# Decay rows kept feature by feature in DRAM, and a v load behind their reads, in gated linear attention with a multiplicative FFN

## The chip, the cores and the metric

One core of one Trainium2 chip runs the kernel. The metric is device microseconds of one execution. The kernel before took 466.35 us, the median of 3 runs (466.15 to 468.48).

## What is computed

Two blocks follow each other. The first is gated linear attention: 4 batches of 8 heads, 768 steps, 48 features. Each head carries a state of 48 x 48:

```python
for t in range(S):
    state = alpha[:, :, t, :, None] * state + einsum('bhd,bhe->bhde', k[:, :, t], v[:, :, t])
    y[:, :, t] = einsum('bhd,bhde->bhe', q[:, :, t], state)
```

The second takes the result as 3072 tokens of 384 features and computes `((x @ w1) * (x @ w2)) @ w3 @ w_out`, with 1024 inner features. All data is float32 (the four weights come as float64).

## The kernel before

**Chunks.** The 768 steps of a batch are cut into 6 chunks of 128, so there are 24 chunks (n = 0 to 23) for all heads at once. Per chunk, alpha, k, q and v are loaded as tiles of 128 steps x 8 heads x 48 features (192 KB each); ScalarE takes the logarithm of alpha (L318, L326), TensorE sums it along the steps (L346, L352, L355), and ScalarE makes two exponentials of the sums, e[:, 0] = exp(-sum) (L361) and e[:, 1] = exp(sum) (L362). e has two buffers. VectorE scales k and q with them (L371). TensorE then turns k and q (L393), makes the scores (L510, later L476), VectorE masks them (L513, L483), and TensorE multiplies scores by v (L536, L436), the state by q (L530, L436), and k by v for the new state (L405), which VectorE adds to the old one (L413, L415).

**Two chunks on one base.** Sums of an even and the odd chunk before it run towards a common point, so that the state needs to be decayed only at even chunks. The even chunks 2, 4, 8, 10, 14, 16, 20 and 22 (those that don't begin a batch) have an entry in `ends`, a DRAM tile of 3 rows of 384 values: row 0 is the first row of exp(-sum) of chunk n (L364), row 1 the last row of exp(sum) of chunk n-1 (L366), row 2 the first row of alpha of chunk n (L322, L333). The product of the three is the decay of each of the 384 features. The state lies with the features on partitions, four heads on partitions 0 to 47 and four on 64 to 111, so the rows have to be turned: they are stored to DRAM, and two loads (L379, one for each half i) read them back with the feature d on the partition and 3 x 4 single values (row m, head pair j) on each. GpSimd multiplies the three (L422, L423) and scales the state: `Ts[0] = T(n-1) * dec` (L424).

**Queues.** All stores to `ends` and the loads from it are issued by GpSimd, in one order with its other work: chunk 3 to 7's v loads (L160), copies of v to the other half of the partitions (L168) and, late in the kernel, other transfers. A store waits for ScalarE's exponential, the loads wait until the three stores have landed, and L422 waits until the loads have landed. SP issues all other transfers, with raw weights (L238) and k and q (L154, L155) in between, each waiting for its buffer.

**Order.** The order of the program is written out by hand in the loop over n (L740 on): what an engine does next is the order in which it is called, with `after_marks`, which lets a piece of work be placed after a marked instruction. `mark["pool"]` is the newest store to `ends` or the newest L424; before chunk 6, chunk n + 2's v is issued after it (L776 to L778). In the first six chunks ScalarE and VectorE also convert the weights from float64 (L246 to L267). From chunk 6 on, the FFN's products (L566), three passes for each product in reduced precision, fill TensorE beside the attention, and from 184 us on they are alone.

Of the kernel before, what the change touches and what calls it, by code (L numbers as in the profile page):

```python
# [10 lines left out]
FP32 = mybir.dt.float32  # L11
# [37 lines left out]
def kernel(  # L49
# [12 lines left out]
    nc = tc.nc  # L62
    B, H, S, D = q.shape
    C = 128
    DM = H * D
    DF = moe_w1.shape[1]
    NCH = S // C
    N = B * NCH
    NP = H // 2
    DP = 64  # L70
# [15 lines left out]
    def pool(name, bufs, stack=ctx, **kw):  # L86
        return stack.enter_context(tc.tile_pool(name=name, bufs=bufs, **kw))
# [7 lines left out]
    dram = pool("dram", 1, space=DRAM)  # L95
# [14 lines left out]
    st, mark = {}, {}  # L110

    def after_marks(*names):
        stack = ExitStack()
        for x in names:
            stack.enter_context(tc.issue_after(mark[x]))
        return stack
# [1 line left out]

    ends = {n: dram.tile([3, DM], FP32, name=f"ends{n}") for n in range(2, N, 2) if n % NCH}
    xd = [dram.tile([DM, TG], FP32, name=f"xd{g}") for g in range(NG)]
    abd = [dram.tile([C, KF, TG], FP32, name=f"abd{g}") for g in range(NG)]

# [11 lines left out]
    def paired(n):  # L136
        return 2 <= n < PAIRED
# [12 lines left out]
    def load_kq(n):  # L150
        if n >= N:
            return
        st["kq", n] = inp.tile([C, 2, H, D], FP32, tag="kq", name="kq")
        nc.sync.dma_start(out=st["kq", n][:, 0], in_=rows(k, n))  # L154
        nc.sync.dma_start(out=st["kq", n][:, 1], in_=rows(q, n))  # L155

    def load_v(n):
        if n < N:
            st["v", n] = vs[n % len(vs)]
            (nc.gpsimd if 2 < n < 8 else nc.sync).dma_start(out=st["v", n][:, :, 0:D], in_=rows(v, n))  # L160
# [37 lines left out]
    decs = [p1.tile([C, 3, NP], FP32, name=f"dec{i}") for i in range(2)]  # L198
# [83 lines left out]
    def fetch(ahead=3):  # L282
        while weights and len(begun) < ahead:
            begun.append(weights.popleft())
            next(begun[-1])
# [17 lines left out]
    def store():  # L303

        while later:
            dst, src = later.popleft()
            nc.sync.dma_start(out=dst, in_=src)

    def last(n):
        return n % NCH == NCH - 1  # L310

    def logs(n):
        if n >= N:
            return
        a = st.pop(("a", n))
        if paired(n):
            if n % 2 == 0:
                nc.scalar.activation(a, a, AF.Ln)  # L318
                st["la", n] = st["la", n + 1] = a
                b, c = divmod(n, NCH)  # L320
                if n in ends:
                    nc.gpsimd.dma_start(out=ends[n][2:3].rearrange("m (h d) -> m h d", h=H), in_=alpha[b:b + 1, :, c * C, :])  # L322
            return
        a = a.rearrange("p h d -> p (h d)")
        la = st["la", n] = work.tile([C, DM], FP32, tag="la", name="la")
        nc.scalar.activation(la, a, AF.Ln)  # L326
        if n >= LATE:

            t = st["la", n] = work.tile([C, 2, DM], FP32R, tag="la2", name="la2", bufs=1)
            nc.scalar.copy(t[:, 0], la)  # L330
            nc.vector.tensor_sub(t[:, 1], la, t[:, 0].bitcast(FP32))
        if n in ends:
            nc.gpsimd.dma_start(out=ends[n][2:3], in_=a[0:1])  # L333

    def decays(n):
        if n >= N:
# [21 lines left out]
    def exponentials(n, lc):  # L358

        e = st["e", n] = work.tile([C, 2, DM], FP32, tag="e", name="e", bufs=2)  # L360
        nc.scalar.activation(e[:, 0], lc, AF.Exp, scale=-1.0)  # L361
        mark["e", n] = nc.scalar.activation(e[:, 1], lc, AF.Exp).ins  # L362
        if n in ends:
            mark["pool"] = nc.gpsimd.dma_start(out=ends[n][0:1], in_=e[0:1, 0]).ins  # L364
        if n + 1 in ends:
            mark["pool"] = nc.gpsimd.dma_start(out=ends[n + 1][1:2], in_=e[C - 1:C, 1]).ins  # L366
        load_ends(n)

    def decayed(n):
# [4 lines left out]
    def load_ends(n):  # L374
        if n not in ends:
            return
        with nc.allow_non_contiguous_dma(reason="single values to partitions"):
            for i in range(2):
                nc.gpsimd.dma_start(out=decs[n // 2 % 2][ds(DP * i, D)].rearrange("d m j -> d (m j)"),  # L379
                                    in_=ends[n].rearrange("m (j i d) -> i d (m j)", i=2, d=D)[i])  # L380

    def transposed(n):
        if n >= N:
# [166 lines left out]
    def load_x(g, queue=nc.sync):  # L550
        st["xT", g] = xp.tile([C, KM, TG], FP32, tag="xT", name="xT")
        queue.dma_start(out=st["xT", g], in_=xd[g].rearrange("(k p) t -> p k t", p=C))
# [171 lines left out]
    with after_marks(("e", 0)):  # L724
        logs(1)
# [14 lines left out]
    for n in range(N + 1):  # L740
        if n > TURNED:
            load_v(n + 2)
        if not 1 < n < FIRST:
            store()
        if n in loads:
            load_x(loads[n])
        if n != 1 and not 2 < n <= FIRST:
            load_a(n + 5)
        raws = (3, 3, 3, 3, 2, 2, 3, 3)[n] if n < 8 else 4
        for m in (n + 3,) * (n <= FIRST) + (n + 4,) * (n >= FIRST):  # L750
            load_kq(m)
            if 2 < n <= FIRST and m == n + 3:
                load_a(n + 5)
            if 1 < n < FIRST:
                store()
            if n < FIRST - 2:
                fetch(raws)
        if FIRST <= n <= TURNED:
            load_v(n + 2)
        if 0 < n <= TURNED:  # L760
            attend_state(n - 1)
        if n < TURNED:
            scores(n)
        else:
            attention(n)
        if ("lc", n + (2 if n == 1 else 3)) in st:
            exponentials(n + (2 if n == 1 else 3), st.pop(("lc", n + (2 if n == 1 else 3))))
        transposed(n + 1)
        if n == 1:
            decays(3)  # L770
            load_a(6)
            with after_marks(("e", 3)):
                logs(4)
        if n == FIRST + 1:
            run(2)
        if n < FIRST:  # L776
            with after_marks("pool"):
                load_v(n + 2)  # L778
        if n - 2 in begin and n > FIRST:
            g, tiles = begin[n - 2]  # L780
            with after_marks(("ms", n), ("qkT", n + 1)):
                split_x(g, 0)
            fill.extend(gate(g, f) for f in tiles)
        if n == FIRST:
            with after_marks("l", ("qkT", n + 1)):
                split_x(0, 0)
            fill.extend(gate(0, f) for f in begin[n - 3][1])
        pieces = ((3, 3, 2, 0) if n > FIRST + 3 else (0, 3, 3, 0))[(n - FIRST) % 4] if n >= FIRST else 0
        if n == 0:
            with after_marks(("qkT", 0)):  # L790
                logs(2)
            decays(2)
            with after_marks(("e", 2)):
                logs(3)
        early, ready = n < FIRST, len(thirds) if n > 2 else n // 2
        marks = (*[("qkT", n + 1)] * (n < N - 1), *[("qk", n + 1), ("ms", n)] * early, *["x3"] * (n - 2 in begin and n > FIRST))
        if n < N - 2 and n != FIRST:
            with after_marks(*marks):
                convert(2 if early else 1, raws)
        advance(n)  # L800
        turn_v(n)
        if n > TURNED:
            st.pop(("x", n - 1))()
        elif n:
            attend(n - 1)
        outer(n)
        if n > FIRST:
            third(ready)
        run(pieces > 0)
        if early:  # L810
            with after_marks(*marks):
                convert(1, raws)
        with after_marks(*[("ms", n)] * (n < 3)):
            decayed(n + 2)
        if not early:
            with after_marks(*[("qkT", n + 1)] * (n < N - 4)):
                logs(n + 4)
        if n == 4:
            load_x(0)
        convert(early and n > 0, raws)  # L820
        run(pieces > 1)
        if n:
            decays(n + 3)
        if n <= FIRST:
            third(ready)
        if 0 < n < FIRST:
            with after_marks(("e", n + 3)):
                logs(n + 4)
        if n == FIRST:
            with after_marks("x3", ("e", n + 3)):  # L830
                convert(2, raws)
        elif n < N - 2:
            convert(n == FIRST - 1 if early else n % 3 == 0, raws)
        if n == FIRST - 1:
            assert len(done) == 2 * KM
        run(pieces > 2)
        if n == N - 3:
            while begun:
                convert(1)
            weights.extend(load_out(j) for j in range(KF))  # L840
            fetch(4)
# [90 lines left out]
```

## Time and profile before

| | |
|---|---|
| median of the runs | 466.35 us |
| the profiled execution, its time | 463.35 us |
| the profiled execution, its span | 461.6 us |
| busy: TensorE, VectorE, ScalarE, GpSimd | 444.5, 362.9, 278.0, 97.6 us |
| GpSimd waits for `dec<-ends` (L422) | 33.4 us in 8 times |
| GpSimd waits for `ends<-e` (L379) | 15.8 us in 7 times |
| DMA issues to landing: `v<-in_v_dram` from GpSimd | x5, 5.4 us |
| `kq<-in_q_dram` from SP | x24, 5.4 us |
| all DMA | 80.38 MB, 149381 packets |

The span runs from the first to the last instruction; the execution's own time is 1.75 us longer. In a line of the timeline the first number is the start, the second the duration in us, and in brackets stands how long the engine was idle before and what ended it. In the chain of waits a line is a piece of the chain that ended last. `SPq` is SP's issue of transfers, PEld is TensorE's load of weights.

### The profile page before, as it was taken

How to read it: one execution, taken by the hardware profiler on the slowest of the kernel's cores; microseconds unless marked ns; L12 is line 12 of the kernel's file. 1: busy time of each engine (PE TensorE's matmuls, PEld its weight loads, DVE VectorE, ACT ScalarE, POOL GpSimd, SP SyncE). 2: the span in 40 equal slices, each digit the busy share in tenths (PEclk: the TensorE clock that was granted, in tenths of full speed). 3: DMA queues.
4: the chain of work that ended last, by engine and by line, in shares of the span. 5: the costliest groups of instructions: out<-in, count | busy, mean ns of one | idle time of the engine just before them, and what ended most of it. 6: DMA issues, size and time to landing. Idle time of an engine off the chain costs nothing.

```text
span 461.6 us, 11168 instructions
## 1 busy us (share of the span) xinstructions
PE 444.5 (96%) x4296; PEld 424.3 (92%) x4296; DVE 362.9 (79%) x578; ACT 278.0 (60%) x544; POOL 97.6 (21%) x186
## 2 busy tenths in 40 slices
PE   4969899999999999999999999999999999999996
PEld 2657699989999999999999999999999999999996
DVE  2878996899868879999997999997543966776671
ACT  4758775857667564998866676764545433333430
POOL 6335152215431460121221202112010000000000
PEclk9979999999999999999999999999999999999999
DMA  9999999999998966658764436412115865665511
GB/s 177 262 191 237 263 222 209 236 209 213 172 197 180 213 165 210 181 190 252 210 211 143 150 127 176 149 51 87 51 53 157 253 201 174 184 184 158 161 51 53
DMA packets 149381, 80.38 MB, mean 174 GB/s; under 512 B 97904, under 2 KB 139120, under 8 KB 149328
## 3 DMA queue, kind: packets, MB, share of 16 engines
q1 hardware_dynamic: 143552, 64.44, 56.4%
q0 software_dynamic: 5776, 15.22, 10.9%
q8 instruction: 34, 0.56, 0.5%
q14 instruction: 19, 0.16, 0.1%
HBM read 57.58 MB, written 22.06 MB: 173 GB/s over the span
## 4 chain that ended last, share of the span: by engine, by line
PE 87%; DVE 4%; DMA 4%; ACT 2%; issue 1%; SPq 0%; DVEq 0%; ACTq 0%
PE bank L566 72%; PE bank L436 5%; DMA kq<-in_q_dram 3%; PE bank L393 3%; PE bank L476 2%; PE bank L405 2%; DMA ac<-in_alpha_dram 2%; PE bank L355 1%; DVE qk L371 1%; PE bank L352 1%; PE bank L536 1%; DVE ms L513 1%; PE bank L510 1%; DVE mant L253 0%; DVE power L254 0%
## 5 line engine op out<-in xcount | busy, mean ns | idle before, releaser
L566 PE MATMUL bank<-x,w 128*128 128x384 f32 x1152 | 209.4, 337 | 0.9 <-DVE ms L483 0.9
L566 PEld LDWEIGHTS bank<-x,w 128*128 128x128 f32 x1152 | 200.3, 188 | 2.3 <-DVE ms L483 1.4
L566 PE MATMUL bank<-w3o,ab 128*128 128x384 f32 x576 | 100.2, 336 | 0.0
L566 PEld LDWEIGHTS bank<-w3o,ab 128*128 128x128 f32 x576 | 99.9, 188 | 0.0
L591 ACT ACTIVATE bank<-bank 128x384 f32<-128x384 f32 x96 | 45.8, 478 | 40.7 <-PE bank L566 40.6
L575 ACT ACTIVATE t<-bank 128x384 f32<-128x384 f32 x64 | 31.3, 494 | 53.9 <-PE bank L566 53.9
L641 POOL DMA_DIRECT2D abd<-ab x45 | 25.8, 573 | 135.2 <-DVE ab L627 115.7
L692 DVE TENSOR_TENSOR ab<-abl,ab 128x1024 fp32r<-128x1024 f32 x24 | 29.4, 1224 | 12.4 <-ACT ab L691 12.3
L691 ACT ACTIVATE ab<-abl 128x1024 fp32r<-128x1024 f32 x24 | 25.5, 1061 | 20.4 <-PE bank L566 18.9
L566 PE MATMUL bank<-wo,w3T 128*128 128x384 f32 x192 | 35.9, 334 | 0.0
L627 DVE TENSOR_TENSOR ab<-bank,r 128x384 f32<-128x384 f32 x44 | 24.4, 553 | 13.5 <-ACT bank L591 6.9
L371 DVE TENSOR_TENSOR qk<-kq,e 128x768 f32<-128x768 f32 x24 | 23.3, 969 | 13.3 <-ACT e L362 8.0
L566 PEld LDWEIGHTS bank<-wo,w3T 128*128 128x128 f32 x192 | 33.5, 188 | 0.0
L395 ACT COPY qkT<-bank 128x512 f32<-128x512 f32 x48 | 26.1, 596 | 8.9 <-PE bank L393 8.9
L577 DVE SCALAR_TENSOR_TENSOR o<-bank,t 128x384 f32<-128x384 f32 x24 | 13.4, 557 | 22.8 <-issue 14.1
L251 ACT ACTIVATE power<-power,rebias 128x512 uint32<-128x512 uint32 (+1 forms) x36 | 25.2, 701 | 8.3 <-DVE power L250 8.2
L693 DVE SCALAR_TENSOR_TENSOR ab<-ab,abl 128x1024 fp32r<-128x1024 f32 x24 | 29.2, 1218 | 0.0
L577 DVE SCALAR_TENSOR_TENSOR r<-bank,t 128x384 f32<-128x384 f32 x40 | 22.0, 552 | 8.7 <-ACT t L575 5.3
L254 DVE SCALAR_TENSOR_TENSOR power<-raw,power 128x512 uint32<-128x512 uint32 (+1 forms) x36 | 23.6, 656 | 4.0 <-ACT power L251 4.0
L253 DVE SCALAR_TENSOR_TENSOR mant<-mant,rest 128x512 f32<-128x512 uint32 (+1 forms) x36 | 24.0, 666 | 2.1 <-ACT rest L246 2.1
L476 PE MATMUL bank<-qkT 48*64 48x128 f32 (+1 forms) x512 | 25.2, 247 | 0.1
L436 PE MATMUL bank<-ms,v 64*64 64x64 f32 (+1 forms) x256 | 24.6, 245 | 0.0
(100 smaller groups left out, 693.7 us busy)
## 6 DMA issues: line engine op xcount, KB each, us to landing
abl<-abd SPq DMA_DIRECT2D x24, 512.0 KB, 4.4
abd<-ab POOLq DMA_DIRECT2D x45, 192.0 KB, 2.9
raw<-in_moe_w_dram SPq DMA_DIRECT2D x64, 128.0 KB, 3.4
raw<-in_moe_w_dram SPq DMA_DIRECT2D x12, 512.0 KB, 5.8
xT<-xd POOLq DMA_DIRECT2D x9, 576.0 KB, 4.8
kq<-in_k_dram SPq DMA_DIRECT2D x24, 192.0 KB, 5.2
kq<-in_q_dram SPq DMA_DIRECT2D x24, 192.0 KB, 5.4
out_dram<-o SPq DMA_DIRECT2D x24, 192.0 KB, 3.5
```

What stands on the lines that cost most here:

```text
L371: mark["qk", n] = nc.vector.tensor_mul(qks[n % 3][:, :, :, 0:D], st.pop(("kq", n)), st.pop(("e", n)).rearrange("p i (h d) -> p i h d", h=H ...
L395: mark["qkT", n] = nc.scalar.copy(qkT[:, :, :, ds(DP * half, DP)], tp[half]).ins
L436: nc.tensor.matmul(to, w, x, start=(at, i) not in first, stop=True, skip_group_check=True)
L476: nc.tensor.matmul(sc[1][to, j, :] if late else sc[0][to, :, j, :], qkT[r, 0, j, ds(DP * late, DP)], q, start=True, stop=True)
L566: nc.tensor.matmul(p, w[part][i], x[part][i], start=start and part == parts[0] and i == 0, stop=stop and part == parts[-1] and i == n - 1, ...
L575: nc.scalar.activation(t, p1, AF.Copy, scale=(1.0 + 1.0 / P) * scale)
L577: nc.vector.scalar_tensor_tensor(to, p2, scale, t, op0=ALU.mult, op1=ALU.add)
L591: nc.scalar.activation(p, p, AF.Copy, scale=1.0 + 1.0 / P)
L641: (nc.gpsimd if late else nc.sync).dma_start(out=abd[g][:, f, :], in_=ab)
L691: nc.scalar.activation(t[:, 0], ab, AF.Copy, scale=1.0 - 2.0 ** -13)
L692: nc.vector.tensor_sub(t[:, 1], ab, t[:, 0].bitcast(FP32))
L693: nc.vector.scalar_tensor_tensor(t[:, 2], t[:, 0].bitcast(FP32), -1.0 - 1.0 / P, ab, op0=ALU.mult, op1=ALU.add)
```

## The change

`ends[n]` gets the shape [2, 48, 3, 4]: half i, feature d, row m, head pair j, so that the 3 x 4 values of one feature lie side by side, 48 bytes. The three stores of a chunk go through one helper, `store_end`, which views the row as (j, i, d) and writes it value by value, 4 bytes each, into its places, 48 bytes apart along d. The program lists such a store as 4 x 96 x 1 (before: 16 pieces of 24 values, or 8 x 48 for the alpha rows of chunks 2 and 4). The loads read 48 rows of 12 values each (before: 48 x 12 x 1). The last load of chunk 2 is marked, and chunk 3's v (issued at n = 1) is placed after it: on GpSimd it now comes behind the two loads of chunk 2, instead of ahead of them. On TensorE, VectorE, ScalarE and SP the order of the instructions is the same; on GpSimd, besides v, one copy of v (L168) changes places with L422 and L423 at chunk 10.

```diff
-    ends = {n: dram.tile([3, DM], FP32, name=f"ends{n}") for n in range(2, N, 2) if n % NCH}
+    ends = {n: dram.tile([2, D, 3, NP], FP32, name=f"ends{n}") for n in range(2, N, 2) if n % NCH}
...
+    def store_end(n, m, row):
+        with nc.allow_non_contiguous_dma(reason="a feature's values side by side"):
+            return nc.gpsimd.dma_start(out=ends[n][:, :, m:m + 1, :].rearrange("i d m j -> m j i d"), in_=row).ins
+
     def logs(n):
...
                 if n in ends:
-                    nc.gpsimd.dma_start(out=ends[n][2:3].rearrange("m (h d) -> m h d", h=H), in_=alpha[b:b + 1, :, c * C, :])
+                    store_end(n, 2, alpha[b:b + 1, :, c * C, :].rearrange("m (j i) d -> m j i d", i=2))
...
         if n in ends:
-            nc.gpsimd.dma_start(out=ends[n][2:3], in_=a[0:1])
+            store_end(n, 2, a[0:1].rearrange("m (j i d) -> m j i d", i=2, d=D))
...
         if n in ends:
-            mark["pool"] = nc.gpsimd.dma_start(out=ends[n][0:1], in_=e[0:1, 0]).ins
+            mark["pool"] = store_end(n, 0, e[0:1, 0].rearrange("m (j i d) -> m j i d", i=2, d=D))
         if n + 1 in ends:
-            mark["pool"] = nc.gpsimd.dma_start(out=ends[n + 1][1:2], in_=e[C - 1:C, 1]).ins
+            mark["pool"] = store_end(n + 1, 1, e[C - 1:C, 1].rearrange("m (j i d) -> m j i d", i=2, d=D))
...
             for i in range(2):
-                nc.gpsimd.dma_start(out=decs[n // 2 % 2][ds(DP * i, D)].rearrange("d m j -> d (m j)"),
-                                    in_=ends[n].rearrange("m (j i d) -> i d (m j)", i=2, d=D)[i])
+                loaded = nc.gpsimd.dma_start(out=decs[n // 2 % 2][ds(DP * i, D)].rearrange("d m j -> d (m j)"),
+                                             in_=ends[n][i].rearrange("d m j -> d (m j)"))
+        if n == 2:
+            mark["dec"] = loaded.ins
...
         if n < FIRST:
-            with after_marks("pool"):
+            with after_marks("pool", *["dec"] * (n == 1)):
                 load_v(n + 2)
```

## The prediction

> **What bounds the kernel now.** I read the page's busy shares first: TensorE 96% of 461.6 us, and the chain that ended last lies on it for 87%. So the table by stretches comes second, to find where TensorE is not the bound. From 58 to 80 us it is busy 22.00 of 22 us, from 80 to 120 us 39.05 of 40, from 120 to 184 us 64.00 of 64; the decays are loaded eight times, at 22, 34, 57.5 and then 72 to 163 us, and all but the first two are waited for in those stretches, which have about 1 us of TensorE idle in all. The first two lie in the first 58 us, where the chain looks different. It is, in the chain of waits between 14 and 60 us (start, us, what):
>
> ```profile
> 26.90 0.35 DVE power L250
> 27.24 0.27 SPq L154
> ...
> 27.56 6.16 DMA kq<-in_q_dram
> ...
> 33.81 0.96 DVE qk L371
> 34.77 1.20 DVE ms L513 x2
> ```
>
> The reader is to see that one q load of 6.16 us, issued when a buffer came free on VectorE, holds the end there, and not the decays. The decays' own waits stand high in the list of waits all the same (us, times, longest):
>
> ```profile
> POOL dec L422 <- DMA dec<-ends: 33.4, 8, 5.8
> ...
> POOL dec L379 <- DMA ends<-e: 15.8, 7, 3.4
> ...
> PE bank L530 <- POOL T L424: 4.0, 1, 4.0
> ```
>
> GpSimd waits 33.4 us for the loads and 15.8 us for the stores before them, but only once does TensorE wait for what comes of it: chunk 2. GpSimd's timeline there, then VectorE's:
>
> ```profile
> 17.15 0.49 POOL L364 DMA_DIRECT2D ends<-e  x1 [4.71 <-ACT e L361]
> 18.29 0.48 POOL L366 DMA_DIRECT2D ends<-e  x1 [0.65 <-ACT e L362]
> 18.77 0.95 POOL L160 DMA_DIRECT2D v<-in_v_dram  x1
> 21.97 1.37 POOL L379 DMA_DIRECT2D dec<-ends  x2 [2.25 <-DMA ends<-e]
> 29.19 0.20 POOL L422 TENSOR_TENSOR dec<-dec 128x4 f32<-128x4 f32 x1 [5.85 <-DMA dec<-ends]
> 29.47 0.88 POOL L423 TENSOR_TENSOR dec<-dec,dec 128x4 f32<-128x4 f32 x1
> 30.43 0.51 POOL L424 TENSOR_TENSOR T<-tmp,dec 128x192 f32<-128x192 f32 x1
> ```
>
> ```profile
> 30.97 0.36 DVE L415 TENSOR_TENSOR T<-bank,T 128x192 f32<-128x192 f32 x1 [0.68 <-POOL T L424]
> ...
> 33.81 0.96 DVE L371 TENSOR_TENSOR qk<-kq,e 128x768 f32<-128x768 f32 x1 [0.56 <-DMA kq<-in_q_dram]
> ```
>
> TensorE stands from 27.0 to 30.99 us for T. VectorE loses 0.68 us to T, and then, after three conversions, still waits 0.56 us for the q load. So an earlier T is worth little there, and a T later than by 0.56 us is paid for.
>
> **Pieces.** Per even chunk, three stores of 16 pieces (8 for the two early alpha rows) and two loads of 48 x 12 = 576 single values become three stores of 4 x 96 = 384 single values and two loads of 48 rows of 48 bytes: 1200 pieces before, 1248 after. The bytes stay. The price of a piece comes from the DMA issues (xcount, KB, median us to landing):
>
> ```profile
> ends<-e POOLq DMA_DIRECT2D x16, 1.5 KB, 3.8
> dec<-ends POOLq DMA_DIRECT2D x16, 2.2 KB, 4.9
> ```
>
> and the issues' durations on GpSimd, 533 ns (store, L364) and 696 ns (load, L379). 560 more pieces go with 1.1 us of landing, 2.0 ns each, and 0.16 us of issue, 0.29 ns each. A load then gains 528 x 2.0 = 1.06 us of landing; two issues gain 528 x 0.29 = 0.15 us each, of which the first one's stands before the second load. The row-0 store, the last of the three and the one that the loads wait for, loses 368 x 2.0 = 0.74 us, its longer issue within it. Store plus loads: +0.74 - 1.06 - 0.15 = **-0.5 us** per even chunk. The row-1 store of the next even chunk stands ahead of T's product at chunks 8, 14 and 20 and costs 0.11 us more there.
>
> No row writes single values to DRAM, so I bound that store from both sides. Below: nothing lost (pieces are free, the loads' 1.1 us were queueing), but then the loads gain nothing either. Above: the program lists the store as 4 x 96, so if the four outer rows are what is spread, one string of 96 values is served where the loads have 576 / 16 = 36 per DMA engine: 96 / 36 x 1.1 = 2.9 us later. I take 0.74 us, since the trace's packet records show 36 values in 46 ns against 12 ns for one 96-byte piece: 1 ns a value on the engine, so even 96 in a string come to 0.1 us there. Of the wider question the Trainium skill, DMA: Bandwidth & Descriptors, says in its section on why a DMA increments its semaphore by 16 that the number of engines is the largest one up to 16 that divides the slowest dimension; by it this store runs on 4 engines. Its rules for kernel authors say that a strided last dimension costs a descriptor per element; by it this change moves that cost from the loads to the stores. Its specifications add that transfers under 512 bytes are read, modified and written; no run here shows that yet. By these three sentences the store is near 2.9 us, and the slow-store rival below is the case.
>
> **The moved v.** Chunk 3's v (192 KB) is issued behind the loads. They no longer stand behind it in GpSimd's queue: they needed 3.0 us from issue to their first packet at chunk 2, 1.5 to 1.7 us at the four late ones after 100 us, and 1.0 us of the difference I put down to v. With the -0.5 us, T would be ready near 29.4 us instead of 30.94. v itself goes out near 23.6 us instead of 18.77; its packets began 3.2 us after the issue before, so it moves about 196 KB from 22-25.5 us to some 26-29 us. Nobody misses it: chunk 3's outer product (L405) comes at 36.55 us, and v's landing takes 5.4 us, so some 7 us cover it. Behind it on GpSimd stands L422, which waits for the loads anyway. But it now meets the q load of 27.56 us. In 26-27 us the DMA share is 0.45 and 74 GB/s (265 GB/s in 27-31 us), so about 190 KB of room is there if v starts at once; I count 0.55 us of it, 140 KB, as usable. The rest, 56 KB at 265 GB/s, is **+0.2 us** on the q load; with none of the room used it is 196 / 265 = +0.74 us.
>
> **What is hidden.** An earlier T leaves the q load next in line, so -1.5 us on T brings nothing beyond the gap of 0.24 us that VectorE has before L253 at 37.49. From chunk 4 on T has cover: 42.4 us against its use at 48.83; for VectorE's L415 at chunks 8, 10, 16 and 22 2.6 to 7.0 us. Only at chunks 14 and 20 (T ends at 115.76 and 158.38, L415 at 116.24 and 158.86) it is 0.48 us, so there a chain longer by more than that is paid for. The order on the other engines is unchanged; at chunk 10 GpSimd only swaps a copy with two products of 0.2 us each.
>
> **Sum.** -0.24 to 0 for the earlier T, +0.2 (0 to +0.74) for v, 0 in the TensorE-bound part: about **+0.2 us**. The profiled execution took 463.35 us, span 461.6 and 1.75 around it, 3.0 below the median of 466.35; added to the median that gives **466.5 us**, own range 466.1 to 467.1.
>
> **Rivals.**
> *Slow stores (0.27).* Strings of single values to DRAM land late. They decide where the store lands more than 1.55 us later: the exponentials have two buffers, so ScalarE's L361 of chunk 4 (22.76 us) waits for the row-0 store of chunk 2, landed at 21.97; 0.79 us cover that, and 0.76 us of idle before L262 the rest. At 2.9 us, 1.35 us pass on, through the 3.3 us that SP waits for L362, to the q load. At chunks 14 and 20 the chain is 2.9 - 1.2 = 1.7 us longer, 0.48 covered: 1.2 us each on VectorE. ScalarE's L361 of chunks 17 and 23 (119.12, 162.43) has 1.9 us of cover against stores issued at 113.40 and 155.68 (landing at 3.8 and 4.8): 1.0 us each. Sum 1.35 + 2.4 + 2.0 = 5.8 at most, since TensorE's queue hides some; I take 4: **470.5 us**. For it: nothing like it is in the trace. Against it: 46 ns a packet.
> *T sets the pace (0.14).* TensorE's 4.0 us of idle are the longest wait of the first 58 us, and its clock shows it:
>
> ```profile
> 27.00:31.00 4.00, 0.02 (x3) 0.01 (x3) 1.22 (x3) 2.65 (x6) 1.65 (x4) 0.82 1.07 265
> 31.00:40.00 9.00, 9.00 (x108) 7.16 (x110) 7.88 (x14) 5.00 (x12) 3.60 (x5) 0.70 0.97 196
> ```
>
> (granted clock, DMA share and GB/s last). With 1.5 us less idle, and the groups L530, L510, L393 and L536 at their later durations (0.66 + 1.16 + 0.66 + 1.09 instead of 1.13 + 2.08 + 1.06 + 1.81, 2.5 us less), up to 4 us could go: I take 2.5, **463.9 us**. The Trainium skill, TensorE: Matmul & The Clock Gate, Part 1, puts the drop at an idle window of about 3.4 us; by it an idle of 2.5 us would keep the clock, and this row, idle 4.0 us and then 0.70, agrees. Against it: the q load ends at 33.72 us whatever TensorE does.
> *The change does not quicken the loads (0.12).* With the same 576 pieces the loads at 163.08 us took 4.0 us until L422, those at 21.97 took 7.2: queueing, not pieces. Then the price of v alone remains, 466.5 to 467.1 us.
> *Forecast (0.47).*
>
> About 0.5% (2.3 us) is what a measurement of this kernel can tell from no change. Faster: most of the T case, 0.12. Slower: the slow stores but for the mild ones, 0.25. The rest, 0.63, is within 0.5%. The range leaves out half of each outer case: **464.2 to 470.0 us**.
>
> **What would show it.** Right: landing of dec<-ends near 3.8 us, of ends<-e near 4.5 us; L424 of chunk 2 ending near 29.4 us, and the q load still followed by L371 at 33.8 to 34.5 us. Wrong: ends<-e above 5.4 us, ScalarE waiting ahead of L361, VectorE waiting for T at chunks 14 and 20 (slow stores); or L371 of 33.81 us coming over 1 us earlier (T sets the pace). A q load issued at another time than 27.5 us would upset the sum altogether.

## The result, and the profile after

The changed kernel took **507.42 us** (median of 6 runs, 504.59 to 510.83) beside 466.25 us for the kernel before: ratio 1.0875 [1.0841, 1.0909]. The profiled execution took 507.91 us, its span is 506.2 us. Of the runs further down, one execution each of `e5_spread`, of `e9_pad64` and of the kernel before beside `e5_spread` ran disturbed and is left out of the medians, and the profile of `e9_pad64`, taken from such a one, is not used.

**Where the 44.6 us of span lie.** The stretch in which only the FFN's last products run (L572 here, L566 before) begins at 228.06 us instead of 183.36 and then lasts as long as before, 274.5 us. So everything was lost in the attention stage, and all along it: VectorE's product of k and q with the exponentials (L375, before L371) starts this much later,

| chunk | 0 | 2 | 4 | 5 | 9 | 15 | 20 | 23 |
|---|---|---|---|---|---|---|---|---|
| before, us | 7.01 | 17.70 | 29.33 | 33.81 | 63.80 | 107.83 | 144.78 | 163.34 |
| after, us | 7.02 | 19.92 | 38.08 | 44.86 | 81.78 | 132.95 | 178.68 | 205.91 |
| later by | 0.0 | 2.2 | 8.8 | 11.0 | 18.0 | 25.1 | 33.9 | 42.6 |

1.8 us per chunk in the mean (1.2 between chunks 9 and 15, 2.9 between 20 and 23), also in the odd chunks, which have no decay to load. The page (DMA queues with packets, MB and the time of the packets as a share of 16 engines' span; then the chain that ended last) points at the transfers. Before:

```profile
q1 hardware_dynamic: 143552, 64.44, 56.4%
q0 software_dynamic: 5776, 15.22, 10.9%
...
PE 87%; DVE 4%; DMA 4%; ACT 2%; issue 1%; SPq 0%; DVEq 0%; ACTq 0%
```

After:

```profile
q1 hardware_dynamic: 143552, 64.44, 55.3%
q0 software_dynamic: 6160, 15.33, 12.2%
...
PE 68%; DMA 18%; SPq 4%; DVE 3%; ACT 3%; issue 2%; POOL 0%; DVEq 0%; ACTq 0%
```

DMA has 18% of the chain, 4% before; most of it is `kq<-in_q_dram` (8% of the span) and `ac<-in_alpha_dram` (7%), transfers that the change does not touch. SP's queue q1 moved the same packets and bytes, but they took 55.3% of 506.2 us, 280 us on each of 16 engines, instead of 56.4% of 461.6 us, 260 us: other transfers' packets got slower. GpSimd's queue q0 moved 15.22 MB before; the 0.11 MB more are 24 stores x 4.6 KB. So by its packets a store of 1.5 KB moves 6 KB: each is 16 packets of 256 bytes and 16 of 128, which, spread evenly, is 96 values on each of the 16 DMA engines, four times the 384. (The records do not name the engine, and the page's line of bytes written to HBM, the chip's DRAM, has 22.06 MB before and after; so whether the repeated values reach DRAM is not shown.)

The DMA issues of after (xcount, KB, median us to landing):

```profile
kq<-in_k_dram SPq DMA_DIRECT2D x24, 192.0 KB, 6.2
kq<-in_q_dram SPq DMA_DIRECT2D x24, 192.0 KB, 7.0
...
ac<-in_alpha_dram SPq DMA_DIRECT2D x18, 192.0 KB, 6.1
...
ends<-e POOLq DMA_DIRECT2D x16, 1.5 KB, 7.4
dec<-ends POOLq DMA_DIRECT2D x16, 2.2 KB, 5.2
```

Before, the last two were 3.8 and 4.9 us, and the loads of SP

```profile
kq<-in_k_dram SPq DMA_DIRECT2D x24, 192.0 KB, 5.2
kq<-in_q_dram SPq DMA_DIRECT2D x24, 192.0 KB, 5.4
...
ac<-in_alpha_dram SPq DMA_DIRECT2D x18, 192.0 KB, 4.4
```

The store itself lands 3.6 us later, the load does not gain, and loads of 192 KB on SP's queue, whose data have nothing to do with the stores, lose 1.0 to 1.7 us each. GpSimd's timeline at chunk 2 has the same places as the one shown of before:

```profile
18.96 0.95 POOL L314 DMA_DIRECT2D ends<-e  x1 [6.08 <-ACT e L365]
22.08 0.95 POOL L314 DMA_DIRECT2D ends<-e  x1 [2.17 <-ACT e L366]
28.44 1.04 POOL L383 DMA_DIRECT2D dec<-ends  x2 [5.40 <-DMA ends<-e]
29.47 0.96 POOL L160 DMA_DIRECT2D v<-in_v_dram  x1
35.57 0.19 POOL L428 TENSOR_TENSOR dec<-dec 128x4 f32<-128x4 f32 x1 [5.14 <-DMA dec<-ends]
...
36.12 0.51 POOL L430 TENSOR_TENSOR T<-tmp,dec 128x192 f32<-128x192 f32 x1
```

From the last store to the load GpSimd now sits 5.40 us (2.25 before), and T is ready at 36.63 us instead of 30.94. But that is not what the kernel waits for there. The chain of waits in the same stretch (start, us, what):

```profile
9.41 9.77 DMA kq<-in_q_dram
...
22.64 9.28 DMA kq<-in_q_dram
...
32.01 0.97 DVE qk L375
```

Two q loads of 9.3 to 9.8 us set the pace. The list of waits agrees (us, times, longest):

```profile
ACT la L330 <- DMA ac<-in_alpha_dram: 39.0, 13, 7.7
...
POOL dec L428 <- DMA dec<-ends: 24.9, 7, 5.1
POOL dec L383 <- DMA ends<-e: 23.5, 5, 5.9
...
DVE qk L375 <- DMA kq<-in_q_dram: 12.9, 3, 8.3
```

ScalarE's wait for alpha went from 9.4 to 39.0 us; GpSimd's two waits for the decays (33.4 and 15.8 us before) hardly changed in sum. Nobody else waits long for T or for a buffer that a store holds: TensorE's wait of 4.0 us for T is gone, VectorE waits 0.4 us for T in all, and ScalarE's first exponential (L365) waits 1.9 us for a store. Once, at chunk 22, the chain that ended last does run through a store: `ends<-e` for 6.82 us from 197.38 us on, 3.79 us for which the profile names no releaser, the loads, and behind them in GpSimd's queue the copies of v (L168), for which TensorE waits until 210.10 us. So a small part of the loss is the stores' own lateness.

**Idle and clock.** The table by stretches over the attention stage (busy us of PE, PEld, DVE, ACT and POOL, then granted clock, DMA share, GB/s), first before, then after:

```profile
12.00:183.40 171.40, 164.40 (x2691) 146.90 (x2688) 145.36 (x256) 117.26 (x257) 58.33 (x100) 0.98 0.96 212
```

```profile
12.00:228.00 216.00, 187.47 (x2691) 162.92 (x2689) 145.92 (x256) 117.34 (x257) 62.04 (x100) 0.89 0.89 171
```

The same 2691 matmuls. TensorE's idle time grew from 7.0 to 28.5 us, +21.5; its busy time from 164.4 to 187.5, +23.1. Together these are the 44.6 us. By the mean clocks, an estimate, 164.4 x 0.98 / 0.89 = 181.0 us, so 16.6 of the 23.1 are the clock; the other 6.5 stay unexplained. Late transfers thus seem to cost twice, once as idle time and once more in the matmuls behind it. The Trainium skill, TensorE: Matmul & The Clock Gate, Part 1, lets the clock drop to half after an idle window of some 3.4 us. The trace of after shows no single idle gap of that length: the clock was 0.50 from 27 to 40 us, behind a stretch (20 to 27 us) with 2.78 us busy of 7, in gaps of 0.94, 1.34 and 1.94 us. VectorE's and ScalarE's work did not grow, GpSimd's by 3.7 us. The DMA engines' rate fell from 212 to 171 GB/s, their share only from 0.96 to 0.89: they move less in the time that they are occupied.

### The profile page after: what moved, and what is told of

It is laid out like the page before. It is cut to its first block, busy times and chain, and to the rows that moved or that the text cites. A ratio compares the mean times of both kernels' runs of the same rounds, so it can differ in the third digit from the quotient of the medians.

```text
span 506.2 us, 11167 instructions
## 1 busy us (share of the span) xinstructions
PE 467.6 (92%) x4296; PEld 440.4 (87%) x4296; DVE 363.4 (72%) x578; ACT 277.8 (55%) x544; POOL 102.1 (20%) x186
## 3 DMA queue, kind: packets, MB, share of 16 engines
q1 hardware_dynamic: 143552, 64.44, 55.3%
q0 software_dynamic: 6160, 15.33, 12.2%
HBM read 57.58 MB, written 22.06 MB: 157 GB/s over the span
## 4 chain that ended last, share of the span: by engine, by line
PE 68%; DMA 18%; SPq 4%; DVE 3%; ACT 3%; issue 2%; POOL 0%; DVEq 0%; ACTq 0%
PE bank L572 59%; DMA kq<-in_q_dram 8%; DMA ac<-in_alpha_dram 7%; PE bank L442 3%; SPq L307 2%; PE bank L482 2%; DMA ends<-e 1%; PE bank L399 1%; DMA xT<-xd 1%; DVE qk L375 1%; DMA kq<-in_k_dram 1%; SPq L154 1%; SPq L238 1%; DVE ms L519 1%; PE bank L542 1%
## 5 line engine op out<-in xcount | busy, mean ns | idle before, releaser
L572 PE MATMUL bank<-x,w 128*128 128x384 f32 x1152 | 209.7, 337 | 4.3 <-ACT t L581 2.5
L572 PEld LDWEIGHTS bank<-x,w 128*128 128x128 f32 x1152 | 200.4, 188 | 6.2 <-ACT t L581 3.1
L572 PE MATMUL bank<-w3o,ab 128*128 128x384 f32 x576 | 100.2, 336 | 0.0
L572 PEld LDWEIGHTS bank<-w3o,ab 128*128 128x128 f32 x576 | 99.9, 188 | 0.0
L375 DVE TENSOR_TENSOR qk<-kq,e 128x768 f32<-128x768 f32 x24 | 23.0, 959 | 22.7 <-DMA kq<-in_q_dram 12.9
L482 PE MATMUL bank<-qkT 48*64 48x128 f32 (+1 forms) x512 | 29.8, 271 | 10.0 <-ACT t L581 7.7
L482 PEld LDWEIGHTS bank<-qkT 48*64 48x64 f32 x512 | 26.3, 150 | 12.2 <-ACT t L581 8.4
L572 PE MATMUL bank<-wo,w3T 128*128 128x384 f32 x192 | 35.8, 334 | 0.0
L572 PEld LDWEIGHTS bank<-wo,w3T 128*128 128x128 f32 x192 | 33.5, 188 | 0.0
L251 ACT ACTIVATE power<-power,rebias 128x512 uint32<-128x512 uint32 (+1 forms) x36 | 25.1, 698 | 10.8 <-DVE power L250 10.6
L442 PE MATMUL bank<-ms,vt 64*64 64x64 f32 (+1 forms) x256 | 29.4, 274 | 1.6 <-POOL vt L168 1.6
L330 ACT ACTIVATE la<-ac 128x384 f32<-128x384 f32 x18 | 9.4, 524 | 39.0 <-DMA ac<-in_alpha_dram 39.0
L442 PE MATMUL bank<-ms,v 64*64 64x64 f32 (+1 forms) x256 | 30.2, 273 | 0.4 <-issue 0.4
```

What stands on the lines that cost most here:

```text
L251: nc.scalar.activation(power, power, AF.Relu, scale=2.0 ** 23, bias=rebias)
L375: mark["qk", n] = nc.vector.tensor_mul(qks[n % 3][:, :, :, 0:D], st.pop(("kq", n)), st.pop(("e", n)).rearrange("p i (h d) -> p i h d", h=H ...
L442: nc.tensor.matmul(to, w, x, start=(at, i) not in first, stop=True, skip_group_check=True)
L482: nc.tensor.matmul(sc[1][to, j, :] if late else sc[0][to, :, j, :], qkT[r, 0, j, ds(DP * late, DP)], q, start=True, stop=True)
L572: nc.tensor.matmul(p, w[part][i], x[part][i], start=start and part == parts[0] and i == 0, stop=stop and part == parts[-1] and i == n - 1, ...
```

## The experiments

Three theories to begin with. **V**: the moved v costs it. **L**: the stores land late, and those that wait for them (loads, T, exponentials) lose it. **H**: the single-value stores hold every other transfer up. V and L can be told from H by moving v alone, and by adding stores that nothing waits for.

**v moved back, and v moved alone.** `e1_v_back` is the changed kernel with v where it was, `e2_v_only` the kernel before with v behind the loads:

```diff
-            with after_marks("pool", *["dec"] * (n == 1)):
+            with after_marks("pool"):
```

> The changed kernel with chunk 3's v where it was before, ahead of the two loads. Theory H (a store of single values to DRAM holds the DMA engines, so that every other transfer that runs beside it lands late; 24 stores for 41.2 us, 1.7 us each): 503 to 510 us, with kq<-in_q_dram still near 7.0 us to landing and ends<-e near 7.4. Theory L (only what waits for these stores is late: the loads behind them, T, and ScalarE's exponentials behind their buffers): the same 503 to 510 us. Theory V (the moved v starts the delay): 466 to 472 us.

> The kernel before with chunk 3's v behind the two loads of chunk 2, and nothing else. Theories H and L: no single-value store, so 465.5 to 467.5 us, with T of chunk 2 ready 1 us or more before 30.94 us and the q load of 27.56 us landing 0 to 0.8 us later than 33.72. Theory V: 500 us or more.

`e1_v_back`: 507.59 us beside 466.37, ratio 1.0883 [1.0829, 1.0938]. `e2_v_only`: 465.88 us, 0.999 [0.9958, 1.0021]. V falls. In the trace of `e2_v_only` TensorE's wait for T shrank from 4.0 to 0.9 us, and the time did not move: VectorE now waited 2.23 us for the q load behind it (0.56 before). So T was not what the first 58 us hung on.

**Idle stores.** `e3_idle_dram` and `e4_idle_sbuf` are the kernel before, untouched, with 24 more stores of 384 single values each, one for each real one, from a row of q, into a tile that nothing reads:

```diff
+    apart = {n: dram.tile([2 * D, 3, NP], FP32, name=f"apart{n}") for n in ends}
...
+                nc.gpsimd.dma_start(out=apart[n][:, m, :].rearrange("x j -> j x"),
+                                    in_=q[0, 0, 0:H, :].rearrange("h d -> (h d)").rearrange("(j x) -> j x", j=NP))
```

(the places of the values are those of the changed kernel, 48 bytes along d and 4 along j; in `e4_idle_sbuf` the target is four partitions of SBUF, 8 bytes apart).

> The kernel before, with its own stores and loads, and beside each store to ends one more store of 4 x 96 single values from a fixed row of q into a DRAM tile that nothing reads; each stands on GpSimd behind the store it doubles (the row-0 one behind the loads), so no instruction waits for its data. Theory H: 490 to 515 us, kq<-in_q_dram near 7 us to landing, packets beside it up to 2 or 3 us long. Theory L: the chain of decays is untouched but for 24 issues of about 1 us on GpSimd, 466 to 471 us, kq<-in_q_dram near 5.4 us.

> As the run with idle stores to DRAM, but the 4 x 96 single values go to 4 partitions of an SBUF tile that nothing reads, 8 bytes apart: the same number of pieces, the same issue on GpSimd, no write to DRAM. Theory H, in the form that writes to DRAM hold the engines: 466 to 470 us, kq<-in_q_dram near 5.4 us. If it is the number of pieces or their issue on GpSimd whatever they write to: as the run to DRAM, 490 us or more. Theory L: 466 to 471 us.

`e3_idle_dram`: 505.23 us, 1.0824 [1.075, 1.0898]. That is +38.9 us from stores without a single waiter, of the change's 41. L falls as the main cause, H stands. Its DMA issues:

```profile
kq<-in_q_dram SPq DMA_DIRECT2D x24, 192.0 KB, 6.9
...
apart<-in_q_dram POOLq DMA_DIRECT2D x24, 1.5 KB, 7.5
```

The q loads land as late as in the changed kernel (7.0), and the idle stores as late as its real ones (7.4). `e4_idle_sbuf`: 493.48 us, 1.0572 [1.049, 1.0654], +27.1. I had expected a write into SBUF to cost little; it does not, so H is not a matter of writing to DRAM alone. (Its stores, 4 x 96 too, also moved four times their bytes: q0 15.37 MB.)

**What is the price made of?** Theory **P**: it grows with the number of values that one DMA engine has to write. Theory **W**: it goes per value written, wherever. `e5_spread` stores the real rows as a list of 384 values 12 bytes apart (no fourfold bytes, but for the two alpha rows of chunks 2 and 4, which the packets show twice; v unmoved, loads 48 x 12 single values as before), `e7_idle_384x1` and `e8_idle_2x192` are `e3_idle_dram` with other shapes, 48 bytes along the longer dimension:

```diff
+    ends = {n: dram.tile([DM, 3], FP32, name=f"ends{n}") for n in range(2, N, 2) if n % NCH}
+                mark["pool"] = nc.gpsimd.dma_start(out=ends[n][:, 0:1].rearrange("x m -> m x"), in_=e[0:1, 0]).ins
...
+                nc.gpsimd.dma_start(out=apart[n][:, m:m + 1, 0].rearrange("x m -> m x"), in_=...)
...
+                nc.gpsimd.dma_start(out=apart[n][:, m, :].rearrange("x y -> y x"), in_=...)
```

(first `e5_spread`, then the idle store of `e7_idle_384x1`, with `apart` of [384, 3, 4], and of `e8_idle_2x192`, with [192, 6, 2]).

> A changed form of the change: ends[n] holds, for each of the 384 features in their own order, its three values side by side, so that a store is 384 single values at one even step of 12 bytes (384 x 1) instead of 4 x 96; loads are 576 single values as before, v stands where it stood before. Theory P (the packet records of the changed kernel show 16 packets of 256 bytes and 16 of 128 for each store, 96 values on each DMA engine, and the time goes with that number: 39 us for 24 x 96 values in the run with idle stores, 17 ns each): if this form puts 24 values on each engine, 24 x 24 x 17 ns = 10 us, so 474 to 482 us. Theory W (each single value written to DRAM costs, 384 a store, however they are spread): 500 to 510 us.

> As the run with idle stores to DRAM, same 384 single values 48 bytes apart and same places, but as 384 x 1. Theory P: 24 instead of 96 values on each engine, 24 x 24 x 17 ns = 10 us, 473 to 480 us. Theory W: 500 to 510 us.

> As the run with idle stores to DRAM, the same 384 single values 48 bytes apart, but as 2 x 192. Theory P: if the packet records show 192 values on each engine, 24 x 192 x 17 ns = 78 us, 530 to 555 us. Theory W: 500 to 510 us.

Beside 465.46 us: `e5_spread` 513.27, 1.1091 [1.1025, 1.1156]; `e7_idle_384x1` 467.03, 1.0043 [1.0009, 1.0077]; `e8_idle_2x192` 503.09, 1.0826 [1.0752, 1.09]. Both theories fall. In `e5_spread` an engine writes 24 values of a store (packets of 96 bytes) and the time is worse than with 96; in `e8_idle_2x192` it writes 192, eightfold bytes in all (q0 15.52 MB), and the time is that of 96. And 384 values a store that cost 47.8 us as real stores cost 1.6 us in `e7_idle_384x1`:

```profile
kq<-in_q_dram SPq DMA_DIRECT2D x24, 192.0 KB, 5.6
...
apart<-in_q_dram POOLq DMA_DIRECT2D x24, 1.5 KB, 4.7
```

GpSimd's queue is no explanation either: in all the runs with idle stores these stand at the same places, and their issue, 0.98 us in `e3_idle_dram`, 1.37 in `e8_idle_2x192` and 0.61 in `e7_idle_384x1`, does not go with the cost.

**Distance and source.** What differs between `e5_spread` and `e7_idle_384x1`, besides that the former's stores are waited for: 12 bytes between values instead of 48 (theory **C**, crowding), and a row of SBUF as source instead of DRAM (theory **B**). `e9_pad64` is `e5_spread`'s idea with every value 64 bytes from the next; `e10_idle_12b`, `e14_idle_24b` (384 idle values from DRAM) and `e12_idle_from_sbuf`, `e16_12b_sbuf` (256 idle values from one row of a constant in SBUF) change distance and source one at a time (the four `apart` lines are those of `e10`, `e14`, `e12` and `e16` in this order, the store that of `e16`):

```diff
+    ends = {n: dram.tile([3, DM, 16], FP32, name=f"ends{n}") for n in range(2, N, 2) if n % NCH}
...
+    apart = {n: dram.tile([DM, 3], FP32, name=f"apart{n}") for n in ends}
+    apart = {n: dram.tile([DM, 6], FP32, name=f"apart{n}") for n in ends}
+    apart = {n: dram.tile([2 * C, 3, NP], FP32, name=f"apart{n}") for n in ends}
+    apart = {n: dram.tile([2 * C, 3], FP32, name=f"apart{n}") for n in ends}
...
+                nc.gpsimd.dma_start(out=apart[n][:, m:m + 1].rearrange("x m -> m x"), in_=signs[0:1].bitcast(FP32).rearrange("m e x -> m (e x)"))
```

> The kernel before with every value of ends 64 bytes from the next (3 x 384 values in rows of 64 bytes, one used): the real stores become 384 single values, 384 x 1, from e's row in SBUF; the loads stay 576 single values. Theory C (what costs is single values written close together, several into the same 64 bytes; 48 bytes apart as 384 x 1 was nearly free, 12 bytes apart was not): 466 to 473 us. Theory B (what costs is single values read one by one from one SBUF partition, or a count over 24 on an engine; the run with 384 x 1 from DRAM had neither): 500 to 515 us.

> The idle store as 384 x 1 from the fixed row of q in DRAM, but 12 bytes apart instead of 48. Theory C: 485 to 515 us. Theory B: 466 to 469 us.

> The idle store as 384 x 1 from the fixed row of q, 24 bytes apart. Theory C, by values within 64 bytes (5.3 at 12 bytes, 2.7 at 24, 1.3 at 48): between 467 and 489, 475 to 482 us. If the step has to be under 16 or 20 bytes to count: 466 to 469 us.

> The idle store as 256 x 1, 48 bytes apart, read from one partition of a constant in SBUF instead of a row in DRAM. Theory C: 466 to 469 us. Theory B: 485 us or more.

> The idle store as 256 x 1 from one partition of the SBUF constant, 12 bytes apart. So far 48 bytes apart: 1 us from DRAM (384 values), 6 us from SBUF (256 values); 12 bytes apart from DRAM 23 us (384 values), which is 15 us for 256. If source and distance add up: 15 + 6 = 21 us, 483 to 491 us. If the source adds nothing: 479 to 483 us. If crowded writes from SBUF are worse than the sum, as the real stores hint (48 us): 493 us or more.

| kernel | values, source, distance | us, before's | ratio | difference |
|---|---|---|---|---|
| e10_idle_12b | 384, DRAM, 12 B | 488.73, 465.89 | 1.0475 [1.0406, 1.0544] | +22.8 |
| e14_idle_24b | 384, DRAM, 24 B | 477.05, 467.07 | 1.0218 [1.0154, 1.0282] | +10.0 |
| e7_idle_384x1 | 384, DRAM, 48 B | 467.03, 465.46 | 1.0043 [1.0009, 1.0077] | +1.6 |
| e16_12b_sbuf | 256, SBUF row, 12 B | 509.82, 468.76 | 1.0877 [1.0845, 1.0908] | +41.1 |
| e12_idle_from_sbuf | 256, SBUF row, 48 B | 471.88, 465.89 | 1.0114 [1.0048, 1.018] | +6.0 |
| e5_spread (real) | 384, SBUF row, 12 B | 513.27, 465.46 | 1.1091 [1.1025, 1.1156] | +47.8 |
| e9_pad64 (real) | 384, SBUF row, 64 B | 477.24, 465.89 | 1.0206 [1.0137, 1.0276] | +11.4 |

(The ratios need not equal the quotient of the two medians shown.) C and B both hold, and not as a sum: 12 instead of 48 bytes costs 21 us more from DRAM, 35 us more from an SBUF row, with fewer values. `e10_idle_12b` and `e7_idle_384x1` differ in nothing but this distance, the issue on GpSimd takes 0.62 and 0.61 us; so it is not the number of pieces or their issue alone that costs. `e12_idle_from_sbuf` and `e9_pad64` came out between the times that C and B had given: source and distance each explain a part. Idle stores from SBUF at 12 bytes, with 256 instead of 384 values, come near to `e5_spread` (41 of 48).

**The fourfold bytes.** `e11_idle_rows` keeps the shape 4 x 96 and the 48 bytes along d, but puts the four rows 4.6 KB apart. `e15_four_stores` is the changed kernel with each store cut into four of 96 values, which write each value once (but for the two alpha rows of chunks 2 and 4):

```diff
+                nc.gpsimd.dma_start(out=apart[n][:, 0:2 * D, m], in_=q[0, 0, 0:H, :].rearrange("h d -> (h d)").rearrange("(j x) -> j x", j=NP))
...
-            return nc.gpsimd.dma_start(out=ends[n][:, :, m:m + 1, :].rearrange("i d m j -> m j i d"), in_=row).ins
+            for j in range(NP):
+                stored = nc.gpsimd.dma_start(out=ends[n][:, :, m:m + 1, j].rearrange("i d m -> m i d"), in_=row[:, j])
+            return stored.ins
```

> The idle store as 4 x 96 again, 48 bytes apart within a row, the four rows 4.6 KB from each other, so that no two different values share 64 bytes; the packet records should show 96 values on each of 16 engines again, each value four times. Theory C, by different values: 466 to 472 us. If the number of values on an engine counts, or the fourfold writing: 495 to 510 us.

> The changed kernel with each store of 4 x 96 issued as four stores of 96 single values, 48 bytes apart in themselves; every value is then written once, 6 of a store by each engine, and the four neighbours of 4 bytes come from stores one after another. Three more issues a store, 66 to 72 in all, 0.5 us each on GpSimd, 1.5 us of them before the loads. If fourfold writing and neighbours written at the same time are what costs: 468 to 480 us. If single values from SBUF cost the same however they are dealt out: 495 us or more.

`e11_idle_rows`: 487.05 us beside 465.89, 1.0439 [1.0362, 1.0516]. No two values are closer than 48 bytes, and still +21.2 us, where the list of 384 at the same distance costs 1.6. That is between the two forecasts: the shape 4 x 96 itself costs some 20 us, the neighbours at 4 bytes the other 18 of `e3_idle_dram`. `e15_four_stores`: 497.7 us beside 467.07, 1.066 [1.0594, 1.0727]: q0 is back at 15.24 MB, but only 10 of the 41 us come back. 96 issues of 0.51 us instead of 24 of 0.98 stand on GpSimd now, and ScalarE's first exponential waits 6.4 us for stores instead of 1.9, so part of the gain may have been spent on a new wait.

**A third of the stores.** `e17_a_third` has `e3_idle_dram`'s idle stores only beside the 8 real stores of row 1 (`if n in ends and m == 1`).

> The idle stores of 4 x 96 to DRAM, 48 and 4 bytes apart, as in the first such run, but only the 8 beside the row-1 stores instead of all 24. If each store has its price: a third of 39 us, 13 us, 476 to 483 us. If only the pile of stores in the first 58 us (where DMA is full) costs: 2 of the 8 fall there, so 468 to 473 us.

474.91 us beside 468.76, 1.0132 [1.0046, 1.0217]: +6.2 us (2 to 10 by the interval), not the 13 of a third, and between the two forecasts. A store costs 0.8 us here and 1.6 in `e3_idle_dram`; the price is not a sum over stores.

**Is there something to gain from the loads?** `e6_wide_loads` is the kernel before with loads of 48 x 3 pieces of 16 bytes from the rows as they are stored (so the decays go to other features than they belong to). `e13_staged` makes that a full kernel, with one buffer fewer for x: GpSimd turns the rows of the exponentials around in SBUF before they are stored in long pieces, and the alpha row is loaded from the input:

```diff
...
-                                    in_=ends[n].rearrange("m (j i d) -> i d (m j)", i=2, d=D)[i])
+                                    in_=ends[n].rearrange("m (i d j) -> i d m j", i=2, d=D)[i])
...
+        nc.gpsimd.tensor_copy(out=stage[rows].rearrange("p (i d j) -> p j i d", i=2, j=NP), in_=row.rearrange("p (j i d) -> p j i d", i=2, d=D))
+        return nc.gpsimd.dma_start(out=ends[n][m:m + 1], in_=stage[last:last + 1]).ins
```

> The kernel before, with the same rows in DRAM, but the loads read 48 x 3 pieces of 16 bytes (four neighbours in a row) instead of 48 x 12 single values; the decays come to other features than their own, so the output is not the reference's, and the values keep their range. Theory P: 36 values on each engine become 9 pieces, 16 loads x 27 fewer x 12 to 17 ns = 5 to 7 us, so 458 to 462 us. If the loads' single values cost nothing, and only the stores' do: 465.5 to 467.5 us.

> The kernel before with no single-value store and a quarter of the loads' pieces: GpSimd copies each row of e into a staging row in the order (i, d, j), stores it in 16 pieces, and the loads read 48 x 2 pieces of 16 bytes; alpha's row comes straight from the input as 48 x 4 single values, ahead of time; x has three buffers instead of four, to make room. 16 copies of some 0.6 us on GpSimd, of which the row-0 one stands before the store that the loads wait for. By the run with wide loads (2.0 to 2.6 us faster) and no crowded writes: 462.5 to 466 us. If the copies or the x buffer cost: 466 to 470 us.

`e6_wide_loads`: 462.92 us beside 465.46, 0.9956 [0.9931, 0.9982], with dec<-ends landing in 3.0 us instead of 4.9. So the loads were worth about 2.5 us. `e13_staged`: 468.73 us beside 467.07, 1.0042 [1.0017, 1.0066]. The copies take a median of 1.04 us each on GpSimd, 16 times, and dec<-ends lands in 4.2 us: the gain is given back, to the copies or to the missing x buffer, which no run tells apart. No version that computes the right decays was faster than the kernel before.

## Why the prediction was wrong

- **The failed step** is the price of the store: I counted it as the store's own lateness, "+0.74 us" with 2.9 us as upper bound, paid by those who wait for the store. The sum has no term for what the store does to the other transfers: it was left at nothing, on no other ground than the 1 ns a value of the next point. That term is nearly the whole result: 38.9 of 41 us (`e3_idle_dram`), with q loads landing in 6.9 us instead of 5.4. With it fell "0 in the TensorE-bound part": chunk 9 was 18.0 us late and the end of the attention stage 44.7, so some 27 us were lost behind it, where TensorE had been busy nearly without a gap and where the chain of after waits for loads instead (7.97 us for one of alpha at 72.37 us).
- **The argument that led there.** "46 ns against 12 ns ... 1 ns a value on the engine" was read from packets that *read* DRAM single values and write 12 neighbours on a partition. (Over all such packets of the trace the 46 are 48 in the median and 86 in the mean.) It says what a packet takes while it is served, and nothing of single writes. In the median even the written packets bear it out, 79 ns for 64 values in the trace of after; but their mean is 305 ns, and the loss lies with the other transfers. `e6_wide_loads` shows that the reads were cheap (2.5 us for 16 loads); the writes were not.
- **The price of a piece**, 2.0 ns, was the difference of two landings, 4.9 and 3.8 us, in one trace. It is no steady quantity: in `e7_idle_384x1`, whose real stores and loads are those of before, both land in 4.0 us.
- **The number of values per engine** was no guide either way. By the rule of the Trainium skill, DMA: Bandwidth & Descriptors, on the largest number of engines that divides the slowest dimension, I took 96 values on four engines for the upper bound. The records show as many packets as 96 values on each of sixteen would make. And 192 (`e8_idle_2x192`) or 24 (`e5_spread`) per engine cost as much. The Trainium skill's other sentence there, that transfers under 512 bytes are read, modified and written, would let all single values cost alike; the runs at 12, 24 and 48 bytes do not. It can still be part of the answer, if writes that fall into the same bytes stand in each other's way; that is an inference, and no run here shows it.
- **The slow-store rival** (470.5 us) had the sign, and its first sign in the profile came true: ends<-e landed at 7.4 us, above 5.4. Its size and mechanism were wrong: it priced the waits of ScalarE's L361 and of VectorE for T at chunks 14 and 20. ScalarE's L365 waited 1.9 us for a store in all, VectorE waited for T not at all at chunk 14 and 0.42 us at chunk 20; at chunk 16 the order had even turned round: GpSimd's product waited 1.5 us for VectorE.
- **v**: predicted +0.2 us, between 0 and 0.74. Alone it made no measurable difference (0.999 [0.9958, 1.0021]); in its trace the q load landed at 34.06 us instead of 33.72. Right.
- **T as pace-setter** falls: `e2_v_only` shortened TensorE's wait for T by 3.1 us and gained nothing. The reading that the q load stands next behind T was right. That a shorter idle time would keep the clock was not: in the trace of before the clock was halved between 29.5 and 30 us, 2.5 to 3.0 us after TensorE stopped, and in that of `e2_v_only` it was 0.64 from 34 to 40 us, where TensorE's longest gap was 2.23 us. The 3.4 us of the Trainium skill are not seen here as one idle gap.
- **The load's gain** of 1.06 us did not appear (4.9 to 5.2 us), presumably since the loads were held up like all transfers; in `e6_wide_loads`, without such stores and with pieces of 16 bytes, the loads landed 1.9 us earlier. The issue got shorter by 0.17 us (696 to 530 ns), 0.15 predicted. The store's issue, which I had at +0.11 us, took 978 ns instead of 533.
- **The range** (464.2 to 470.0) and the chance of 0.25 for slower came from a bound that looked only at waiters. "The bytes stay" was wrong as well: by the packet records they became four times as many.

**Still open**: why values written close to each other, or from one SBUF row, hold up the other transfers; why the price per store falls when there are fewer; why a target in SBUF costs 27 us too. The trace of after has packets of 192 bytes on SP's queue that take up to 2.7 us instead of the median of 15 ns (0.4 us at most before), but not what they wait for, the DMA engine or the memory behind it.

## What to carry to other kernels

A small transfer is priced not only by who waits for it: ask what its pieces do to all the other transfers, and if the trace has no transfer of that kind, add one that nothing waits for and see what the rest loses. Moving single values from the reading to the writing side is no neutral exchange: here 16 loads of 576 scattered reads were worth 2.5 us, and 24 stores of 384 scattered writes cost 41. Where single values must be written, write them as one long list and far apart (48 bytes: 1.6 us from DRAM, 6 us from an SBUF row; 12 bytes: 23 and 41 us); the real rows so written, 64 bytes apart, still cost 11 us (`e9_pad64`).

## What the hardware showed that was not expected

- By the packet records a store of 4 x 96 single values moved four times its bytes, one of 2 x 192 eight times (q0 15.22 to 15.33 and 15.52 MB), as many as 96 and 192 values on each of 16 DMA engines; the two of 8 x 48 in `e5_spread` moved them twice (16 packets of 192 bytes each), and a list of 384 x 1 once, 24 on each. So for the outer lengths 4, 2 and 8 the repetition was 16 divided by it; the 8 x 48 of before, stored in pieces of 192 bytes, was moved once. The page's bytes written to HBM do not show the repetition. The issue on GpSimd took 0.98, 1.37 and 0.61 us.
- With 24 stores of 1.5 KB, 0.04 MB of 80 MB, written value by value, the rate of all transfers in the attention stage was 171 instead of 212 GB/s.
- Half of the loss was not idle time but longer busy time of TensorE, 23.1 of 44.6 us, most of it (16.6, an estimate) by the lower clock: 0.89 instead of 0.98 over the attention stage.
